# An attention and mixture-of-experts kernel: two experts of the first batch move from the step loop to the slot loop

## The chip, the cores and the metric

The kernel runs on one core of a Trainium2 chip. The metric is the device time of one execution in microseconds; the time before is the median of three runs. The profile is one further execution, recorded by the hardware profiler. Engines are named as in the profile: PE is TensorE, DVE VectorE, ACT ScalarE, POOL GpSimd, SP the engine that issues nearly all DMAs.

## The reference, cut to what matters

```python
q_assign = argmax(q_n @ c_n.T); k_assign = argmax(k_n @ c_n.T)
mask = q_assign[..., :, None] == k_assign[..., None, :]
attn = softmax(where(mask, q @ k.T / sqrt(D), -1e9)) @ v      # 4 batches, 8 heads, 768 x 64
x = attn.transpose(0, 2, 1, 3).reshape(4 * 768, 512)
P = exp(x @ w_gate - max)                                     # 3072 x 8
for _ in range(8):                                            # rows, then columns, made to sum to one
    P /= P.sum(1, keepdims=True) + 1e-9
    P /= P.sum(0, keepdims=True) + 1e-9
    P *= N / E
for e in range(8):
    out += P[:, e:e+1] * (relu(x @ w1[e]) @ w2[e])            # w1 512 x 1024, w2 1024 x 512
```

All is float32. The kernel makes the expert products from pairs of float16 numbers (a high part and the low rest), three matmuls for one product.

## The kernel before, in words

**Attention.** A `Planner` (L61) orders this part in Python while the program is traced: each piece of work is a generator that yields the engine it wants and a cost, and the ready piece with the lowest key (`KEYS`, L488, by stage and head) goes next on its engine; `PATIENCE` says how long an engine may be kept for a piece of lower key, `RELUCT` how much an alternative engine is held back. Within this part the largest weights of the first two experts are estimated too: `scan_early` (L1147) loads each matrix in pieces of 512 columns and sums absolute values on ACT (`total`, L298), and `early_weights` (L1221) makes the first two weight pairs of expert 0.

**Steps.** The first batch then runs in the loop over t at L1582: 32 steps, one for each expert and pair of 128-column blocks of the hidden layer. A step has seven positions m = 0 to 6. At each, `layer1` (L1398) makes one of the seven products of Strassen's scheme (Winograd's variant) for layer 1, 6 matmuls of 384 columns into one of two PSUM tiles `h_ps`; these two are used in turn, some twice before they come free. `layer2` (L1540) makes the plain layer 2 of the step before at positions 1 to 6, 6 matmuls of 512 columns at each, into `o_ps`, reading the weight tile `wb` of the step before. `make_w` (L1507) makes the weights of the step after, at positions 1 to 6: a scaling of the raw first matrix on ACT (L1512), sums on POOL, high parts on ACT (L1516) and low parts on POOL (L1517), at position 3 the high half of `wb` on ACT (L1499 in `second_matrix`), at position 4 the high and low parts of the sums (L1522 on ACT, L1524 on POOL), at 5 and 6 the low half of `wb` on DVE (L1502). `store_w` (L1532) writes both tiles to memory, for the later batches. Besides, one raw pair is scanned on ACT for the scales of a later expert, and from t = 8 the input of the second batch is split (`next_x`, L1346). The results of layer 1 go through `m1` (ACT, L1411), combinations on DVE (L1401), ReLU high parts `hh` on ACT (L1610) and low parts `hl` on DVE (L1613, one position later). At an expert's end `gated` (L1554) adds `o_ps` times the gate to the tile `acc`, 512 columns at a time.

The order of instructions on each engine is the order in which they are traced: `keep_order` pins it after each position. Tiles come from pools with a fixed number of buffers; a tile whose pool has none left takes a buffer whose last readers are done, so its first writer waits for them. Those that matter here:

```python
wap = pool("wap", 3)                    # L1278, first-layer weights of a pair
ps_h = pool("ps_h", 2, space=PSUM)      # L1282
wbp = pool("wbp", 3, ax)                # L1460, second-layer weights of a pair
sump = pool("sump", 1, ax)              # L1461
rawp = pool("rawp", 8, ax)              # L1463
```

**Slots.** Batches 2 to 4 run in 24 slots, one for each batch and expert, four pairs of 28 products in all. Layer 1 of slot n stands beside layer 2 of slot n - 1, which is done with seven products too (`layer2b`, L1778): 252 matmuls of 256 columns in three PSUM tiles pa, pb, pc, with evictions on DVE (`evict`, L1768, two of 256 columns for three row groups, or one). `plan_slot` (L1732) says at which position each high half (ACT, L1696), low half (DVE, L1700) and sum (POOL, L1681) is made. The weights come from memory; in the first eight slots the sums of the second matrix are made as well (`second_sums` to `second_low`, L1719).

Of the kernel before, what the change touches and what calls it, by code (L numbers as in the profile page):

```python
# [22 lines left out]
P = 128  # L23
# [37 lines left out]
class Planner:  # L61
# [6 lines left out]
    PATIENCE = {'PE': 0.0, 'ACT': 0.0, 'POOL': 0.26, 'SP': 0.0, 'DVE': 0.0}  # L68
# [96 lines left out]
def attn_moe_kernel(  # L165
# [138 lines left out]
    NP2 = NF // 2  # L304
    NI = E * NP2
# [28 lines left out]
    with ExitStack() as actx:  # L334
# [153 lines left out]
        KEYS = dict(load=-99.6, scale=-39.4, hilo=-210.9, split0=-186.4, split1=-28.7, split2=-30.4, assign=-39.2, place=-336.7, chain=-64.9, ones=-461.5, max=-25.1, rows=-30.6, exp=0, values=64.8, out=6.0, batch=29.5, group=76.9, vsum=-28.1, group0=-123.5, inputs=-41.6, first=1000)  # L488
# [3 lines left out]
        RELUCT = [4.75, -0.72, 2.33, 16.21, 0.34, 0.01, 0.02, 5.4, -0.46, 3.06, 0.07]  # L492
# [654 lines left out]
        def scan_early(e):  # L1147
            if e:
                yield ev["scales", e - 1]
            for f in range(NF):  # L1150
                yield ev["v", NF * (e + 1) - 4 + f]
                if f == 0:
                    am8 = sm.tile([P, 2, NF], F32, name="am8", bufs=1)
                for m in range(2):
                    yield SP, 0.625
                    t = sm.tile([P, 512], F32, name="scan0", bufs=1)
                    scan_load(e, f, f + 1, m, t)
                    yield plan.copied(1.1) - plan.now.time
                    yield ACT, 0.62
                    total(am8[:, m, f : f + 1], t, t)  # L1160
            am2 = sm.tile([P, 2], F32, name="am2", bufs=1)
            yield DVE, 0.15
            nc.vector.tensor_reduce(out=am2, in_=am8, axis=AX, op=ALU.max)
            yield t_x
            yield from weight_scale(e, am2, misc_tile, sm)
            t_x.put(plan)
            ev["scales", e].set(plan)

# [85 lines left out]
        for e in range(2):  # L1254
            plan.spawn(scan_early(e), urgency("values", NF * (e + 2) - 4))
# [26 lines left out]
    ps_h = pool("ps_h", 2, space=PSUM)  # L1282

# [171 lines left out]
    before = iter(())  # L1455

    with ExitStack() as ax:
# [3 lines left out]
        sump = pool("sump", 1, ax)  # L1461
        junkp = pool("junkp", 1, ax)
        rawp = pool("rawp", 8, ax)  # L1463
        accp = pool("accp", 1, ax)
# [3 lines left out]
        def load_raw(idx):  # L1468
            e, f2 = divmod(idx, NP2)
            fs = slice(f2 * 2 * P, (f2 + 1) * 2 * P)  # L1470
            t = rawp.tile([P, 2048], F32, name="raw")
            nc.sync.dma_start(out=t[:, 0:1024].rearrange("p (c f) -> p c f", c=NC), in_=w1[e, :, fs].rearrange("(c p) f -> p c f", p=P))
            nc.sync.dma_start(out=t[:, 1024:2048].rearrange("p (j m) -> p j m", j=2), in_=w2[e, fs, :].rearrange("(j p) m -> p j m", p=P))
            raws[idx] = t
# [17 lines left out]
        def first_matrix(idx):  # L1492
            raw = raws[idx][:, 0:1024]
            return raw, raw.rearrange("p (k c t f) -> p t k c f", k=2, c=KC, t=2), sump.tile([P, 4, KC, P], F32, name="s1w")
# [59 lines left out]
        def gated(e, acc):  # L1554
            gates_ = gate_values(0, e)

            def done(i, ps):
                gate = gates_[:, i : i + 1]
                if e == 0:
                    nc.vector.tensor_scalar(out=acc[:, i], in0=ps, scalar1=gate, scalar2=None, op0=ALU.mult)  # L1560
                else:
                    nc.vector.scalar_tensor_tensor(out=acc[:, i], in0=ps, scalar=gate, in1=acc[:, i], op0=ALU.mult, op1=ALU.add)
                if e == E - 1 and i % 2 == 1:
                    nc.scalar.dma_start(out=out_v[0][:, i - 1 : i + 1], in_=acc[:, i - 1 : i + 1])
# [3 lines left out]
        AHEAD = 7  # L1568
# [9 lines left out]
        acc = accp.tile([P, NT, DO], F32, name="acc")  # L1578
        scans = {i - 5: (i,) for i in range(8, NI)}
        loads = {0: (), 1: (4, 5), 2: (6, 7, 8), 3: (9, 10)}  # L1580
        loaded = {}
        for t in range(NI):  # L1582
# [317 lines left out]
```

## Time and profile before

| | before |
|---|---|
| median of 3 runs | 2285.46 us (2285.12 to 2286.17) |
| the profiled execution | 2284.72 us |
| its span, first to last instruction | 2282.8 us |
| mean granted clock of TensorE | 0.993 |
| PE busy | 2240.6 us, 98% |
| DVE, ACT, POOL busy | 1644.5, 1143.5, 1118.2 us |

A step or a slot is found in the timeline of PE by its matmuls: 384 columns into `h_ps` are layer 1, 512 columns into `o_ps` layer 2 of a step, 256 columns into pa, pb or pc layer 2 of a slot. Consecutive matmuls overlap in the records, so the distance of starts is the time that counts.

### The profile page before, as it was taken

To read this page: it belongs to the slowest core of one execution; us is meant where nothing else is said; L and a number is where in the kernel's file an instruction comes from. 1 tells how busy PE (TensorE), PEld (TensorE's weight loads), DVE (VectorE), ACT (ScalarE), POOL (GpSimd) and SP (SyncE) were. 2 spreads that over 40 slices of the span, in tenths; PEclk is the share of its full clock that TensorE was granted. 3 is DMA by queue.
4 is the path that set the end of the run, shared out by engine and by line. 5 is a ranking of instruction groups with operands and counts; after the bars stand their busy time and mean duration, and the time that the engine had idled before them with its cause. 6 is when DMAs were issued, how large, how long until landed. Compare 5 with 4: busy or idle time off the path is not lost.

```text
span 2282.8 us, 39661 instructions
## 1 busy us (share of the span) xinstructions
PE 2240.6 (98%) x15491; PEld 1459.8 (64%) x15491; DVE 1644.5 (72%) x2777; ACT 1143.5 (50%) x2107; POOL 1118.2 (49%) x997
## 2 busy tenths in 40 slices
PE   6999999999999999999999999999999999999999
PEld 3455554445555555567777777777777777777777
DVE  7988878567666766588788877776676666666666
ACT  7777786555666665354444443333334333333332
POOL 3676787845555655376566653233332333232223
PEclk7999999999999999999999999999999999999999
DMA  5345453365545543586766664544444554344433
GB/s 125 86 102 160 103 143 98 124 222 181 196 169 190 184 145 106 204 296 212 224 221 217 237 221 167 177 143 131 151 159 136 189 166 135 130 130 139 137 122 102
DMA packets 226860, 369.78 MB, mean 162 GB/s; under 512 B 73800, under 2 KB 163824, under 8 KB 226160
## 3 DMA queue, kind: packets, MB, share of 16 engines
q1 hardware_dynamic: 226240, 365.67, 50.3%
q8 instruction: 121, 1.98, 0.4%
q10 hardware_dynamic: 432, 1.57, 0.2%
q14 instruction: 67, 0.55, 0.1%
HBM read 272.22 MB, written 80.62 MB: 155 GB/s over the span
## 4 chain that ended last, share of the span: by engine, by line
PE 92%; DVE 6%; ACT 2%; issue 1%; DMA 0%; SPq 0%; DVEq 0%; ACTq 0%
PE h_ps L1387 38%; PE pb L1800 12%; PE pa L1800 8%; PE pc L1800 8%; PE av_ps L1004 5%; PE o_ps L1548 4%; PE o_ps L1549 4%; PE o_ps L1547 4%; PE max_ps L849 2%; PE exp_ps L945 2%; PE exp_ps L946 2%; DVE mrt L853 2%; PE misc_ps L1045 1%; PE misc_ps L630 1%; DVE qH L683 0%
## 5 line engine op out<-in xcount | busy, mean ns | idle before, releaser
L1387 PEld LDWEIGHTS <-wa 128*128 128x128 f16 x5376 | 525.9, 98 | 303.6 <-issue 6.2
L1800 PEld LDWEIGHTS <-ho 128*128 128x128 f16 x5940 | 580.7, 98 | 139.8 <-DVE ho L1700 2.6
L1387 PE MATMUL h_ps<-xsT,wa 128*128 128x384 f16 x3072 | 581.8, 326 | 1.2 <-DVE xsT L324 0.6
L1387 PE MATMUL h_ps<-xsB,wa 128*128 128x384 f16 x2304 | 437.8, 326 | 1.3 <-DVE B L1401 0.6
L1681 POOL TENSOR_TENSOR B<-B,B 128x768 f32<-128x768 f32 x96 | 197.2, 2057 | 468.3 <-DVE ho L1700 426.6
L1700 DVE TENSOR_TENSOR ho<-B,ho 128x768 f16<-128x768 f32 x283 | 344.6, 1218 | 0.0
L1846 ACT ACTIVATE B<-B 128x384 f32<-128x384 f32 x288 | 149.7, 520 | 371.1 <-DVE B L1401 369.8
L1800 PE MATMUL pb<-w2o,ho 128*128 128x256 f16 x2556 | 324.8, 273 | 1.0 <-DVE C L1776 1.0
L1401 DVE SCALAR_TENSOR_TENSOR u<-h_ps,m 128x384 f32<-128x384 f32 x256 | 141.4, 552 | 245.4 <-PE h_ps L1387 242.4
L1696 ACT CAST ho<-B 128x768 f16<-128x768 f32 x283 | 226.8, 824 | 15.1 <-POOL B L1681 14.4
L970 POOL TENSOR_TENSOR psum<-psum,pe 128x512 f32<-128x512 f32 x160 | 208.2, 1317 | 43.5 <-ACT pe L952 40.2
L853 DVE TENSOR_REDUCE mrt<-max_ps 128x1 f32<-128x512 f32 (+1 forms) x288 | 188.7, 682 | 42.8 <-PE max_ps L849 41.4
L1800 PE MATMUL pc<-w2o,ho 128*128 128x256 f16 x1692 | 215.9, 273 | 1.5 <-DVE ho L1700 1.2
L1800 PE MATMUL pa<-w2o,ho 128*128 128x256 f16 x1692 | 215.1, 273 | 0.0
L1681 POOL TENSOR_TENSOR B<-B,T 128x768 f32<-128x768 f32 x48 | 95.5, 1991 | 206.0 <-DVE ho L1700 206.0
L952 ACT ACTIVATE pe<-exp_ps 128x512 f32<-128x512 f32 x288 | 164.9, 597 | 57.9 <-PE exp_ps L946 52.1
L1411 ACT ACTIVATE m<-h_ps 128x384 f32<-128x384 f32 x128 | 62.6, 489 | 191.6 <-PE h_ps L1387 181.7
L1844 ACT ACTIVATE B<-h_ps 128x384 f32<-128x384 f32 x96 | 47.1, 490 | 211.4 <-PE h_ps L1387 211.4
L1549 PE MATMUL o_ps<-wb,hl 128*128 128x512 f16 x384 | 145.5, 379 | 0.0
L1548 PE MATMUL o_ps<-wb,hh 128*128 128x512 f16 x384 | 145.5, 379 | 0.0
L1547 PE MATMUL o_ps<-wb,hh 128*128 128x512 f16 x384 | 145.5, 379 | 0.0
L1610 ACT ACTIVATE hh<-c 128x384 f16<-128x384 f32 x128 | 66.9, 523 | 143.3 <-DVE c L1401 142.0
(278 smaller groups left out, 3279.6 us busy)
## 6 DMA issues: line engine op xcount, KB each, us to landing
wa<-w1d SPq DMA_DIRECT2D x98, 896.0 KB
w2o<-w2d SPq DMA_DIRECT2D x168, 512.0 KB
raw<-in_moe_w SPq DMA_DIRECT2D x60, 512.0 KB
w1d<-wa SPq DMA_DIRECT2D x30, 896.0 KB
r<-in_moe_w SPq DMA_DIRECT2D x32, 512.0 KB
w2d<-w2s SPq DMA_DIRECT2D x32, 512.0 KB
w2d<-wb SPq DMA_DIRECT2D x96, 128.0 KB
scan<-in_moe_w SPq DMA_DIRECT2D x32, 256.0 KB
```

The source lines that it names most:

```text
L853: nc.vector.tensor_reduce(out=t["mr"][:, i0 : i0 + ni, ni - 1], in_=ps.rearrange("p (x c) -> p x c", x=ni), axis=AX, op=ALU.max)
L952: nc.scalar.activation(pe, ps.rearrange("p (x c) -> p x c", x=ni), AF.Exp, scale=SCALE)
L970: (nc.gpsimd if e == POOL else nc.vector).tensor_tensor(out=st[:, o : o + N0], in0=old[o], in1=part, op=ALU.add)
L1387: nc.tensor.matmul(ps[:, 0:HB], wa[:, w_, a, c, :], x[:, x_, c, :], start=(first and s_ == 0), stop=(s_ == len(steps) - 1), skip_group_che ...
L1547: nc.tensor.matmul(po[i], hh[:, t, ti], wbh[:, t], start=(first and t == 0), stop=False)
L1548: nc.tensor.matmul(po[i], hh[:, t, ti], wbl[:, t], start=False, stop=False)
L1549: nc.tensor.matmul(po[i], hl[:, t, ti], wbh[:, t], start=False, stop=(last and t == 1))
L1681: nc.gpsimd.tensor_tensor(out=t, in0=d[a], in1=d[c], op=ALU.subtract)
L1696: nc.scalar.copy(t[:, 0], blocks[n, g][o])
L1700: nc.vector.tensor_tensor(out=t[:, 1], in0=blocks[n, g][o], in1=t[:, 0], op=ALU.subtract)
L1800: nc.tensor.matmul(ps[:, q], h[:, h_, f, q * P : (q + 1) * P], w[:, 2 * g + f, w_], start=(first and g == 0 and s_ == 0 and q % 2 == 0), s ...
L1846: rests.append(lambda: nc.scalar.activation(c, c, AF.Relu))
```

## The change

Experts 6 and 7 of the first batch become the first two of now 26 slots (`slots`), the step loop runs 24 steps. The four pairs of each of the two experts get their weights from a generator `later`, which has a raw buffer and a tile of sums of its own, takes its `wa` and `wb` tiles from the same pools `wap` and `wbp` as the steps, and is advanced at positions 0 to 5 of each step from t = 2. The scales of experts 0, 1, 6 and 7 are found in the attention part, in pieces of 1024 columns, and the numbers of the planner are others. The first batch is now summed in the four tiles of quarters that the slots use. In the last slot one high and low half move ahead by one position, and a part of pb lies in another PSUM tile.

```diff
-    PATIENCE = {'PE': 0.0, 'ACT': 0.0, 'POOL': 0.26, 'SP': 0.0, 'DVE': 0.0}
+    PATIENCE = {'PE': 0.0, 'ACT': 0.0, 'POOL': 0.36, 'SP': 0.13, 'DVE': 0.15}
...
+    STD = E - 2
+    FROM = 3
+    EARLY = (0, 1) + tuple(range(STD, E))
...
-        KEYS = dict(load=-99.6, scale=-39.4, hilo=-210.9, split0=-186.4, split1=-28.7, split2=-30.4, assign=-39.2, place=-336.7, chain=-64.9, ones=-461.5, max=-25.1, rows=-30.6, exp=0, values=64.8, out=6.0, batch=29.5, group=76.9, vsum=-28.1, group0=-123.5, inputs=-41.6, first=1000)
+        KEYS = dict(load=168.2, scale=-46.7, hilo=-287.8, split0=-114.4, split1=-46.3, split2=-43.3, assign=-14.6, place=-445.3, chain=-118.2, ones=-454.9, max=-25.6, rows=-104.8, exp=0, values=64.2, out=14.4, batch=-159.5, group=213.1, vsum=-19.7, group0=-215.1, inputs=-292.7, first=1000, scan=-0.4)
...
-        RELUCT = [4.75, -0.72, 2.33, 16.21, 0.34, 0.01, 0.02, 5.4, -0.46, 3.06, 0.07]
+        RELUCT = [25.22, -7.8, 9.65, -7.07, 0.47, 11.56, 2.41, 13.4, 0.64, 12.77, -2.71]
...
+        am8s = {e: sm.tile([P, 2, NP2], F32, name=f"am8_{e}", bufs=1) for e in EARLY}
+
+        def scan_early(m):
+            for j, e in enumerate(EARLY):
+                for f in range(NP2):
+                    yield ev["v", NP2 * j + FROM + f]
+                    yield SP, 0.8
+                    t = sm.tile([P, 1024], F32, name=f"scan{m}", bufs=1)
+                    scan_load(e, 2 * f, 2 * f + 2, m, t)
+                    yield plan.copied(1.7) - plan.now.time
+                    yield ACT, 1.05
+                    total(am8s[e][:, m, f : f + 1], t, t)
+                ev["scan", e, m].set(plan)
...
-        rawp = pool("rawp", 8, ax)
-        accp = pool("accp", 1, ax)
+        rawp = pool("rawp", 7, ax)
...
-        def gated(e, acc):
+        def gated(e):
...
+                j, q = divmod(i, 3)
+                for r, name in enumerate((("C11", "C21"), ("C12", "C22"))[j]):
+                    o, y = totals[name][:, q], ps[:, r * HD : (r + 1) * HD]
...
-        AHEAD = 7
+        AHEAD = 6
...
+        def later():
+
+            for idx in range(NB, NI):
+                e = idx // NP2
+                raws[idx] = raw_ = rawp.tile([P, 2048], F32, name="rawx", bufs=1)
+                fill_raw(raw_, idx)
+                for _ in range(7):
+                    yield
+                wa, wb = wt = w_tiles()
+                raw, A, S_ = first_matrix(idx)
+                nc.scalar.activation(raw, raw, AF.Copy, scale=s1[:, e : e + 1])
+                yield
+                sums(S_, A[:, 1, 0], A[:, 1, 1], A[:, 0, 0], A[:, 0, 1], nc.gpsimd)
+                for o, a in ((A22, A[:, 0, 1]), (slice(A11, A12 + 1), A[:, 1])):
+                    nc.scalar.copy(wa[:, 0, o], a)
+                yield
+                for o, a in ((A22, A[:, 0, 1]), (slice(A11, A12 + 1), A[:, 1])):
+                    nc.vector.tensor_tensor(out=wa[:, 1, o], in0=a, in1=wa[:, 0, o], op=ALU.subtract)
+                yield
+                second = second_matrix(idx, wb)
+                step(second)
+                yield
+                nc.scalar.copy(wa[:, 0, 3:7], S_)
+                yield
+                for o in (0, 2):
+                    nc.gpsimd.tensor_tensor(out=wa[:, 1, 3 + o : 5 + o], in0=S_[:, o : o + 2], in1=wa[:, 0, 3 + o : 5 + o], op=ALU.subtract)
+                step(second)
+                yield
+                step(second)
+                raws.pop(idx)
+                yield
+                store_w(idx, wt)
+                yield
...
-        for t in range(NI):
+        for t in range(NB):
...
                 if m:
                     step(making)
+                if m < 6 and t > 1:
+                    step(extra)
                 if m:
                     step(before)
...
-                if t == NI - 1:
-                    reload_x(1, RIGHT[m])
...
-    slots = [(b, e) for b in range(1, B) for e in range(E)]
+    slots = [(0, e) for e in range(STD, E)] + [(b, e) for b in range(1, B) for e in range(E)]
...
+                elif n == NS - 1 and (o, g) == ("T1", 1):
+                    h, l = 2, 3
...
-        if b == 1:
+        if n < E:
...
-                tiles[CHAINS[i]] = ps_y.tile([P, 4, HD], F32, name=CHAINS[i])
+                ps = ps_y.tile([P, 4, HD], F32, name=CHAINS[i])
+                tiles[CHAINS[i]] = [ps[:, q] for q in range(3)]
+                if n == NS - 1 and CHAINS[i] == "pb":
+                    tiles["pb"][2] = h_tile()[:, 0:HD]
```

## Rows read from the trace of the kernel before

**Rows 1.** The page, busy time, share of the span and instructions of each engine.

```profile
PE 2240.6 (98%) x15491; PEld 1459.8 (64%) x15491; DVE 1644.5 (72%) x2777; ACT 1143.5 (50%) x2107; POOL 1118.2 (49%) x997
```

**Rows 2.** Windows by stage: length, busy us (instructions), granted clock, DMA share, GB/s.

```profile
0.00:60.00 60.00, 39.74 (x192) 19.76 (x193) 44.12 (x106) 43.59 (x77) 21.85 (x36) 0.80 0.53 123
60.00:478.40 418.40, 407.15 (x2669) 206.08 (x2668) 329.73 (x637) 298.95 (x711) 316.50 (x381) 1.00 0.44 115
...
543.00:958.50 415.50, 415.50 (x2217) 216.64 (x2215) 261.80 (x429) 242.59 (x402) 211.96 (x220) 1.00 0.51 168
...
987.20:2249.30 1262.10, 1261.62 (x9662) 944.74 (x9661) 917.64 (x1426) 504.91 (x830) 510.82 (x307) 1.00 0.51 171
2249.30:2282.80 33.50, 27.98 (x254) 24.46 (x251) 17.72 (x34) 5.93 (x8) 15.43 (x7) 0.99 0.41 126
```

**Rows 3.** Timeline of PE, one step: start us, us, engine, line, tiles.

```profile
819.35 1.14 PE L1387 MATMUL h_ps<-xsB,wa 128*128 128x384 f16 x6
820.33 1.14 PE L1387 MATMUL h_ps<-xsT,wa 128*128 128x384 f16 x6
...
822.60 1.14 PE L1387 MATMUL h_ps<-xsB,wa 128*128 128x384 f16 x6
...
833.95 1.14 PE L1387 MATMUL h_ps<-xsB,wa 128*128 128x384 f16 x6
```

**Rows 4.** Timeline of PE, one pair of a slot, from its first product to the next.

```profile
1508.78 1.14 PE L1387 MATMUL h_ps<-xsB,wa 128*128 128x384 f16 x6
...
1522.48 1.14 PE L1387 MATMUL h_ps<-xsB,wa 128*128 128x384 f16 x6
```

**Rows 5.** Timeline of PE and of DVE in the tail, idle time before in brackets.

```profile
2256.77 1.92 PE L1800 MATMUL pc<-w2o,ho 128*128 128x256 f16 x16 [1.22 <-DVE ho L1700]
...
2278.65 0.81 PE L1800 MATMUL pb<-w2o,ho 128*128 128x256 f16 x6 [0.97 <-DVE C L1776]
...
2253.41 0.48 DVE L1776 SCALAR_TENSOR_TENSOR C<-pa,gates,C 128x256 f32<-128x256 f32 x1 [2.66 <-PE pa L1800]
```

**Rows 6.** Line 298, scans in attention and in a step; waits of PE.

```profile
L298 ACT ACTIVATE scan<-scan x32: 612/630/682, 150.0 to 371.6; 128x512 f32<-128x512 f32 x32
...
806.32 1.05 ACT L298 ACTIVATE junk<-raw 128x1024 f16<-128x1024 f32 x1
...
PE exp_ps L945 <- ACT pe L952: 3.4, 6, 1.0
```

**Rows 7.** Windows of two single steps.

```profile
804.76:819.35 14.59, 14.59 (x79) 7.62 (x78) 8.43 (x14) 8.98 (x15) 7.51 (x8) 1.00 0.46 118
...
833.95:848.54 14.59, 14.59 (x79) 7.63 (x78) 10.63 (x17) 8.98 (x15) 7.51 (x8) 1.00 0.26 92
```

**Rows 8.** Timeline of ACT in the step from 804.76 and the start of the next.

```profile
811.98 1.14 ACT L1499 ACTIVATE wb<-raw,s 128x1024 f16<-128x1024 f32 x1
...
814.74 1.03 ACT L1522 CAST wa<-s1w 128x1024 f16<-128x1024 f32 x1
816.58 0.52 ACT L1610 ACTIVATE hh<-c 128x384 f16<-128x384 f32 x1 [0.81 <-DVE c L1401]
...
820.53 0.49 ACT L1411 ACTIVATE m<-h_ps 128x384 f32<-128x384 f32 x1 [0.52 <-PE h_ps L1387]
```

**Rows 9.** Timeline of DVE in the same step.

```profile
807.45 1.01 DVE L324 SCALAR_TENSOR_TENSOR xst<-xqB,sx,xst 128x768 f16<-128x768 f32 x1
...
816.46 0.95 DVE L1613 SCALAR_TENSOR_TENSOR hl<-c,hh 128x384 f16<-128x384 f32 x1
...
818.90 0.54 DVE L1401 SCALAR_TENSOR_TENSOR c<-h_ps,u 128x384 f32<-128x384 f32 x1
...
819.84 0.74 DVE L1502 SCALAR_TENSOR_TENSOR wb<-raw,s,wb 128x512 f16<-128x512 f32 x1
```

**Rows 10.** Windows where the steps begin.

```profile
478.00:484.00 6.00, 4.08 (x25) 1.98 (x23) 4.85 (x8) 4.10 (x9) 1.40 (x2) 0.96 0.67 221
484.00:490.30 6.30, 5.73 (x31) 2.14 (x31) 4.84 (x7) 2.70 (x4) 0.00 (x0) 0.50 0.46 187
```

More of the change, by code (lines that the diff above doesn't have):

```diff
@@ L1145, in out_batch, with early_scale @@
             t_x.put(plan)
[L1147 to L1160, printed above, removed]
+        am8s = {e: sm.tile([P, 2, NP2], F32, name=f"am8_{e}", bufs=1) for e in EARLY}
[10 more added lines that the diff above has]
+                ev["scan", e, m].set(plan)
+        def early_scale(e):
+            for m in range(2):
+                yield ev["scan", e, m]
             am2 = sm.tile([P, 2], F32, name="am2", bufs=1)
             yield DVE, 0.15
-            nc.vector.tensor_reduce(out=am2, in_=am8, axis=AX, op=ALU.max)
+            nc.vector.tensor_reduce(out=am2, in_=am8s[e], axis=AX, op=ALU.max)
             yield t_x
@@ L1167, in scan_early @@
             ev["scales", e].set(plan)
+            if e != EARLY[-1]:
+                plan.spawn(early_scale(EARLY[EARLY.index(e) + 1]), plan.now.key + 100.0)
         def two_tiles():
@@ L1253, in attn_moe_kernel @@
         plan.spawn(first_x(), urgency("inputs", nheads))
-        for e in range(2):
-            plan.spawn(scan_early(e), urgency("values", NF * (e + 2) - 4))
+        for m in range(2):
+            plan.spawn(scan_early(m), urgency("scan", 8))
+        plan.spawn(early_scale(0), urgency("scan", 8))
         plan.spawn(early_weights(), urgency("values", nheads - 12))
@@ L1282, in attn_moe_kernel @@
     ps_h = pool("ps_h", 2, space=PSUM)
+    accp = pool("accb", 1)
     def h_tile():
@@ L1455, in attn_moe_kernel, with total_tile @@
     before = iter(())
+    totals = {}
+    def total_tile(name):
+        return accp.tile([P, 3, HD], F32, name=name, bufs=2 if name == "C21" else 1)
     with ExitStack() as ax:
@@ L1577, in attn_moe_kernel @@
         plan.unpin()
-        acc = accp.tile([P, NT, DO], F32, name="acc")
-        scans = {i - 5: (i,) for i in range(8, NI)}
-        loads = {0: (), 1: (4, 5), 2: (6, 7, 8), 3: (9, 10)}
+        scans = {i - 5: (i,) for i in range(8, NB)}
+        def later():
[30 more added lines that the diff above has]
+                yield
+        extra = later()
+        for name in ("C11", "C21", "C12", "C22"):
+            totals[name] = total_tile(name)
+        loads = {0: (), 1: (4, 5), 2: (6, 7, 8), 3: (9,)}
         loaded = {}
-        for t in range(NI):
+        for t in range(NB):
             e, f2 = divmod(t, NP2)
@@ L1585, in attn_moe_kernel @@
                 po = []
-            for idx in loads.get(t, (t + AHEAD,) if t + AHEAD < NI else ()):
+            for idx in loads.get(t, (t + AHEAD,) if t + AHEAD < NB else ()):
                 load_raw(idx)
-            if 0 < t < NI - 1:
+            if 0 < t < NB - 1:
                 wts[t + 1] = w_tiles()
                 making = make_w(t + 1, wts[t + 1])
-            if t + 2 >= NI:
+            if t + 2 >= NB:
                 loaded[t + 2] = load_wa((t + 2) % NI)
@@ L1648, in attn_moe_kernel @@
             wts.pop(t - 1, None)
-            before = layer2(po, hh, hl, wt, f2 == 0, f2 == NP2 - 1, gated(e, acc) if f2 == NP2 - 1 else None)
-        for x in (sink, inputs, scanning):
+            before = layer2(po, hh, hl, wt, f2 == 0, f2 == NP2 - 1, gated(e) if f2 == NP2 - 1 else None)
+        for x in (sink, inputs, scanning, extra):
             for _ in x:
@@ L1765, in attn_moe_kernel, with evict @@
     LAST = {3: ("C11", 0, 0), 4: ("C22", 1, 1), 5: ("C12", 0, 1), 6: ("C21", 1, 0)}
-    totals = {}
-    def evict(e, ps, gates_, into, begun, qs=range(3)):
+    def evict(n, e, ps, gates_, into, begun, qs):
         for q in qs:
@@ L1792, in layer2b @@
                 if name not in totals:
-                    totals[name] = accp.tile([P, 3, HD], F32, name=name, bufs=2 if name == "C21" else 1)
+                    totals[name] = total_tile(name)
             count = 0
@@ L1811, in layer2b @@
                         if count in ready:
[L1812 removed]
+                            evict(n, e, ps, gates_, INTO[i], begun, ready[count])
                         if count in ready and e == E - 1:
```

36 lines of the change are left out of this document (17 added, 19 removed).

## The prediction

> **What bounds the kernel now.** I read the share of busy time first: TensorE is busy 98% of the span, VectorE 72%, ScalarE and GpSimd half [rows 1]. Then the same by stage: from 543 to 958.5 us (first batch's steps) and from 987.2 to 2249.3 us (slots) TensorE is idle 0.0 and 0.5 us; its idle time is in the attention part, at the two joints and in the tail [rows 2]. So in steps and slots the time is the number of matmuls, and anything else costs nothing as long as it does not hold TensorE up. Third, the timeline of TensorE: a step goes from one first product to the next in 14.60 us (819.35 to 833.95) [rows 3], the same piece of a slot, one pair of column blocks, in 13.70 us (1508.78 to 1522.48) [rows 4].
>
> **What the change removes.** Two experts are eight steps, which become eight pairs in slots: 8 x (14.60 - 13.70) = **-7.2 us**. Layer 1 is the same in both; layer 2 loses an eighth of its columns. The filling and draining of the slots' two-stage order happens once, before and after. A new batch boundary now lies inside the slots; there are two there already and all idle time of that stage is 0.5 us [rows 2], so the third costs at most 0.3 us, which I take.
>
> **The tail.** TensorE waits 1.22 us in the chain pc for a low half on VectorE, which stands behind six evictions that begin at 2253.41, and 0.97 us before the last six matmuls, for the eviction of their own tile [rows 5]. The change moves that low half one place ahead, where VectorE was idle 2.66 us, and gives the third part of pb a buffer of its own. Both waits should go; of the second I keep 0.9 us, since the last eviction must still follow the one before it: **-2.1 us**. If a new wait took their place I would lose just that, so the ends are 0 and -2.2.
>
> **The attention part.** The scans for scales grow from two experts to four: 32 loads and 32 sums as before, of twice the width. A sum of 512 columns took 0.63 us, one of 1024 takes 1.05 [rows 6], so ScalarE gets 32 x 0.42 = 13.4 us more, in a stage where it is busy 299 of 418 us [rows 2]. TensorE waited for ScalarE's exponentials only 3.4 us in all [rows 6]. Keys, reluctances and patience of the planner change too, so the whole order there is new, on SP and GpSimd queues as well. That can't be costed instruction by instruction. Bounds: TensorE is idle 11.2 us from 60 to 478 us, so a better order gains at most that (the first 60 us, with 20.3 idle, could give some more); a loss is bounded by the 13.4 us if all of it lay on the chain. The nearest row, the 3.4 us, says little of it shows: I take **0**, with -6 to +6 for the range.
>
> **The weights of the two experts.** Here I see the price. Their first, low and sum parts are made by a generator that runs beside the steps from t = 2: fifteen pieces for a pair, six pieces a step, thus 2.5 steps a pair, done in step 21. The work itself has room: ScalarE is busy 9.0 us of 14.6, GpSimd 7.5, VectorE 8.4 to 10.6 [rows 7], and a pair adds about 4.1 us of ScalarE in 2.5 steps. But pool wbp keeps three tiles, and the change leaves it so. From position 3 of step t all three are taken: layer 2 of the pair t-1 reads one to the end of the step, the pair t is in the second, and t+1 is written into the third. Only at positions 0 to 2 is one free. The new pair needs a fourth tile from its piece 11 (high half, on ScalarE) until its store, piece 15. The order on each engine is fixed, so whoever comes too late holds up its whole queue.
>
> *Odd pairs of the sequence* (first, third, ...): piece 11 falls on position 4, so ScalarE waits till the last layer 2 matmul of the step. Put on the step that ends at 819.35 [rows 3, 8]: high half 1.14 us to 820.6, the queued hh 0.52 to 821.2, the new sum copy 1.03 to 822.2, the next hh to 822.7, then m1, 0.49, to 823.2. The product of position 2 adds onto the bank that m1 reads, and would have begun at 822.60 [rows 3]: **0.7 us** late. Its store is issued at position 2 of the next step, and the next regular high half then waits a little for it, under cover.
>
> *Even pairs*: piece 11 falls on position 1 and finds the free tile, but the store is piece 15, at position 5. So the regular high half at position 3 (at 811.98 in the row) finds none until about 819.5. Then ScalarE: high half to 820.6, hh to 821.2. VectorE stood meanwhile at the low part that needs this hh (816.46 in the row): that to 821.7, the low half of the weights (0.74) to 822.5, and only then the combination that frees the bank, 0.54, to 823.1 [rows 8, 9]. TensorE wanted that bank at 820.33 [rows 3]: **2.8 us** late, and 3.8 where a split of the next batch's input (1.01 us on VectorE) stands at the same position [rows 9].
>
> Four pairs of each kind: 4 x 0.7 + 4 x (2.8 to 3.8), that is 14.0 to 18.0; I take **+16 us**. No row of before shows this wait, since there the third tile always came free in time; the lower end is 0, if a cover that I don't see exists, and the upper one adds a 2.8 us stall for each odd pair as well, if the regular pair after it gets the later of two buffers: 27 to 29.
>
> **The clock.** Between 478 and 484 us TensorE was busy 4.08 of 6 us, and from 484 to 490.3 the granted clock was 0.50, the level of 1.2 GHz [rows 10]; such a dip loses half of its length, some 3.2 us. Whether single gaps of 2.8 us in dense work bring one, no row shows; the gaps of 1.22 and 0.97 us in the tail did not (0.99 there [rows 2]). Ends: none, or four, 13 us. The surroundings are denser than in that row, so I take about one, **+3 us**.
>
> A rule for pieces stands in the Trainium skill, Perfetto Trace Analysis, Optimizing Scalar/DVE Operations: where ScalarE and VectorE are not saturated but cause bubbles elsewhere, broken-up instructions may finish sooner. By it the change would come out at the first rival's time. Another section of the same page, Optimization Strategy, says that the same gap repeated on the engine that should be saturated can mean that a buffer for the next tile is missing; that is the forecast's mechanism, and no row of before shows such a gap.
>
> **Sum.** -7.2 + 0.3 - 2.1 + 0 + 16 + 3 = +10.0. The profiled execution took 2284.72 us (span 2282.8 and 1.9 around it), 0.7 under the median of 2285.46; 2284.7 + 10.0 = 2294.7, said as **2295 us**. Other work that I cost at nothing: evictions of the steps, 12 halves for 6 rows at each expert's end, on a VectorE that is busy 63% in the steps; scans of sixteen pairs instead of twenty-four; the 2.3 MB of loads and stores that each new pair adds on SP, which runs half a step ahead.
>
> **Rivals.** (a) *No buffer wait*: the pieces are at most 1.14 us, ScalarE has 5 us free a step, so they slip in; then only the gains stay: 2284.7 - 9.0 = 2275.7. For it: the flat 14.60 of all steps. Against it: four tiles alive in three buffers. It decides where the new store lands before position 3 or the high half falls after the step's end. Chance 0.20. (b) *Waits as forecast, but the new order in attention gains 6 to 11 us*: of the 11.2 us idle there most goes; 2284 to 2289, about no change. Chance 0.15. (c) *Waits also after odd pairs, and a clock dip with most stalls*: +11 and +10 on the forecast, 2305 to 2316. Chance 0.12. (d) The forecast, with attention within some us, 2289 to 2303: 0.53.
>
> **How the numbers follow.** About 0.2%, 4.6 us, is what a measurement of this kernel can tell from no change. Faster by that is below 2280.9: (a) and a little of (b), 0.21. The band to 2290.0: most of (b) and the low end of (d), 0.17. Slower: the rest, 0.62. The range goes from 2276, in the middle of (a), to 2306, which leaves out most of (c) and the lower half of (a). The likeliest case's own range is 2289 to 2303.
>
> **What would show it.** Steps 3 to 21 no longer flat at 14.60: in each five, one of about 15.3 and one of 17.4 to 18.4, with TensorE's wait put down to a VectorE combination or to m1 on ScalarE, and ScalarE's high half of wb waiting for the o_ps matmuls. Slots at 13.70; no gaps in pc and pb of the tail. I am wrong if the steps stay flat, if the first product of step 0 comes more than 6 us off 478.4, or if the granted clock falls inside the steps more than once.

## The result: slower by 1.4%, and the profile after

| | before | after |
|---|---|---|
| median of 6 runs each | 2285.29 us | 2318.82 us (2314.52 to 2320.05) |
| ratio, with its 95% interval | | 1.0144 [1.0134, 1.0154] |
| profiled execution / span | 2284.72 / 2282.8 us | 2315.78 / 2314.0 us |

The direction was forecast, the size was not: 2295 us was said, and 2318.8 lies above the range, which ended at 2306. The profiled execution after lies 3.0 us under its median, the one before 0.6 under; so the medians differ by 33.5 us, and the account below is of the 31.2 us by which the two spans differ. In the kernel after the lines have moved: layer 1 is L1398, the combinations on VectorE L1412, the high and low halves of wb L1516 and L1519, hh and hl L1665 and L1668, the stores L1553 and L1555, the new low sums L1623.

First the busy time of each engine, the page's first part, beside [rows 1]:

```profile
PE 2239.8 (97%) x15713; PEld 1481.2 (64%) x15713; DVE 1690.7 (73%) x2846; ACT 1153.2 (50%) x2095; POOL 1175.5 (51%) x1027
```

TensorE's busy time is 0.8 us less than before, the span 31.2 us more: the loss is idle time, or time at a lower clock. The windows of steps and slots (columns as in [rows 2]) say where:

```profile
543.00:882.50 339.50, 309.03 (x1599) 157.36 (x1597) 233.56 (x379) 196.58 (x321) 210.57 (x202) 0.97 0.59 196
882.50:2314.00 1431.50, 1426.34 (x10921) 1068.11 (x10919) 1029.22 (x1604) 566.22 (x930) 578.00 (x352) 1.00 0.52 172
```

The steps, where [rows 2] had not one idle microsecond from 543 us on, now have 30.5 in 339.5, at a clock of 0.97. From first product to first slot took 480.1 us before; with eight steps of 14.60 us [rows 3] less it would be 363.3, and it is 402.4 (480.08 to 882.49). Call the difference, 39.1 us, the **excess** of the steps. The rest went as forecast: the slots went from 1324.3 to 1431.5 us, 107.2 for eight pairs of 13.70 us (109.6) and a tail shorter by 2.1; the first product of step 0 came at 480.1 against 478.4. In sum +1.7 + 39.1 - 116.8 + 107.2 = +31.2.

What the steps wait for, from the waits of TensorE and from ScalarE's writes of the tile wb with what ended the idle time before them (us, times):

```profile
PE h_ps L1398 <- DVE c L1412: 24.7, 8, 8.1
PE h_ps L1398 <- DVE u L1412: 5.2, 5, 1.5
```
```profile
  DMA w2d<-wb: 49.2, 7
  PE o_ps L1566: 13.6, 5
```

ScalarE's high halves of wb, which waited for nothing before, stood idle 62.8 us: 13.6 for layer 2 of the step before, as forecast, but 49.2 for a **store** of the tile to land. Of these seven waits four, 18.9 us, are those of the regular pair after an odd one, which the forecast had as "a little", under cover; the other three, 30.3 us, come after even pairs, where the forecast had layer 2. Two steps after even pairs show the two kinds, in a timeline of the engines:

```profile
587.97 1.14 PE L1398 MATMUL h_ps<-xsB,wa 128*128 128x384 f16 x6
588.17 1.15 ACT L1516 ACTIVATE wb<-raw,s 128x1024 f16<-128x1024 f32 x1 [6.28 <-PE o_ps L1566]
591.50 1.14 PE L1398 MATMUL h_ps<-xsT,wa 128*128 128x384 f16 x6 [2.40 <-DVE c L1412]
...
661.65 1.72 DVE L1519 SCALAR_TENSOR_TENSOR wb<-rawx,s,wb 128x512 f16<-128x512 f32 x1
664.98 2.26 POOL L1623 TENSOR_TENSOR wa<-s1x,wa 128x512 f16<-128x512 f32 x2
666.81 1.14 PE L1398 MATMUL h_ps<-xsB,wa 128*128 128x384 f16 x6
667.27 0.33 SPq L1553 DMA_DIRECT2D w1d<-wa  x1
667.69 2.63 SPq L1555 DMA_DIRECT2D w2d<-wb  x3
672.65 1.15 ACT L1516 ACTIVATE wb<-raw,s 128x1024 f16<-128x1024 f32 x1 [9.53 <-DMA w2d<-wb]
674.24 0.56 DVE L1668 SCALAR_TENSOR_TENSOR hl<-c,hh 128x384 f16<-128x384 f32 x1 [10.23 <-ACT hh L1665]
676.05 2.08 PE L1398 MATMUL h_ps<-xsT,wa 128*128 128x384 f16 x6 [8.10 <-DVE c L1412]
```

In the first, at 587.97 (after the first even pair), the high half follows the last o_ps matmul, TensorE stands idle 2.40 us and the step takes 17.39, 2.8 over 14.60: the forecast's mechanism, nearly to the tenth. In the second the regular pair after an even one takes over the buffer of the *new* pair. Its wb was complete at 663.4. But its store stands behind the store of its wa, in one queue, and that waits for GpSimd's new low sums, done at 667.2. Three pieces are then issued to 670.3, the buffer is free at 672.6, the queue of ScalarE and the one of VectorE behind it start again, and TensorE has stood idle 8.10 us.

The same gap comes back every fifth step: 2.40, 8.10, 7.34 and 3.75 us at position 1 of steps 7, 12, 17 and 22. The Trainium skill (Perfetto Trace Analysis, Optimization Strategy) says that such consistent bubbles on the engine that should be saturated can mean that there is no room for the next tile; here the trace agrees, and the experiments test it.

Around the three longer gaps the clock fell, by the windows there:

```profile
671.40:681.70 10.30, 5.65 (x16) 2.41 (x17) 6.28 (x11) 5.90 (x9) 5.22 (x6) 0.50 0.97 319
756.80:763.60 6.80, 2.99 (x9) 1.38 (x10) 5.52 (x10) 6.41 (x10) 2.37 (x2) 0.50 1.04 351
845.50:848.90 3.40, 3.40 (x10) 1.28 (x9) 3.40 (x5) 1.56 (x3) 2.87 (x3) 0.50 0.42 169
```

TensorE was busy 12.0 us at 0.50, the level of 1.2 GHz, so the clock cost 6.0 us. After the gap of 2.40 us it stayed at full speed.

The tail's two waits [rows 5] are gone; the same places in the timeline of TensorE, with no idle time ahead of them:

```profile
2288.80 2.13 PE L1858 MATMUL pc<-w2o,ho 128*128 128x256 f16 x18
2290.76 1.47 PE L1858 MATMUL pb<-w2o,w2s 128*128 128x256 f16 x12
...
2308.45 1.47 PE L1858 MATMUL pb<-w2o,ho 128*128 128x256 f16 x12
2309.76 0.82 PE L1858 MATMUL h_ps<-w2o,ho 128*128 128x256 f16 x6
```

### The profile page after: what moved, and what is told of

The parts are those of the page before. It is cut to its first block, busy times and chain, and to the rows that moved or that the text cites. A ratio compares the mean times of both kernels' runs of the same rounds, so it can differ in the third digit from the quotient of the medians.

```text
span 2314.0 us, 40227 instructions
## 1 busy us (share of the span) xinstructions
PE 2239.8 (97%) x15713; PEld 1481.2 (64%) x15713; DVE 1690.7 (73%) x2846; ACT 1153.2 (50%) x2095; POOL 1175.5 (51%) x1027
## 4 chain that ended last, share of the span: by engine, by line
PE 85%; DVE 7%; ACT 2%; POOL 2%; DMA 2%; issue 1%; SPq 1%; DVEq 0%; ACTq 0%; POOLq 0%
PE h_ps L1398 34%; PE pb L1858 13%; PE pa L1858 9%; PE pc L1858 9%; PE av_ps L1007 5%; PE exp_ps L948 2%; PE max_ps L852 2%; PE exp_ps L949 2%; PE o_ps L1564 2%; PE o_ps L1565 2%; PE o_ps L1566 2%; DVE mrt L856 1%; DVE wb L1519 1%; DMA w2d<-wb 1%; PE misc_ps L1048 1%
## 5 line engine op out<-in xcount | busy, mean ns | idle before, releaser
L1398 PEld LDWEIGHTS <-wa 128*128 128x128 f16 x5376 | 526.3, 98 | 327.6 <-issue 24.0
L1858 PEld LDWEIGHTS <-ho 128*128 128x128 f16 x6444 | 630.3, 98 | 148.5 <-DVE ho L1754 0.8
L1398 PE MATMUL h_ps<-xsT,wa 128*128 128x384 f16 x3072 | 583.8, 327 | 30.5 <-DVE c L1412 24.2
L1735 POOL TENSOR_TENSOR B<-B,B 128x768 f32<-128x768 f32 x104 | 215.7, 2076 | 522.9 <-DVE ho L1754 479.4
L1398 PE MATMUL h_ps<-xsB,wa 128*128 128x384 f16 x2304 | 437.6, 326 | 2.4 <-ACT m L1422 1.3
L1754 DVE TENSOR_TENSOR ho<-B,ho 128x768 f16<-128x768 f32 x307 | 374.9, 1221 | 4.9 <-ACT ho L1750 4.9
L1858 PE MATMUL pb<-w2o,ho 128*128 128x256 f16 x2748 | 349.7, 273 | 0.0
L1412 DVE SCALAR_TENSOR_TENSOR u<-h_ps,m 128x384 f32<-128x384 f32 x256 | 141.3, 552 | 214.0 <-PE h_ps L1398 213.8
L1750 ACT CAST ho<-B 128x768 f16<-128x768 f32 x307 | 246.3, 825 | 18.1 <-POOL B L1735 17.4
L1858 PE MATMUL pa<-w2o,ho 128*128 128x256 f16 x1836 | 233.4, 273 | 0.0
L1412 DVE SCALAR_TENSOR_TENSOR B<-h_ps,u 128x384 f32<-128x384 f32 x208 | 114.8, 552 | 48.9 <-PE h_ps L1398 48.1
L1007 PE MATMUL av_ps<-pe,vn 128*64 128x512 f32 (+1 forms) x768 | 134.4, 492 | 0.0
L949 PE MATMUL exp_ps<-qX 98*128 98x256 f16 (+1 forms) x384 | 120.4, 328 | 0.0
L1735 POOL TENSOR_TENSOR T<-B,B 128x768 f32<-128x768 f32 x52 | 109.5, 2107 | 4.1
```

What stands on the lines that cost most here:

```text
L949: nc.tensor.matmul(o, t["k2"][0:98, ki], t["qa"][0:98, a:z], start=False, stop=True)
L1007: nc.tensor.matmul(av[o, a:z], vn[:, i, :], heads[t]["pe", c][:, i - i0], start=(i == 0), stop=False, skip_group_check=True)
L1398: nc.tensor.matmul(ps[:, 0:HB], wa[:, w_, a, c, :], x[:, x_, c, :], start=(first and s_ == 0), stop=(s_ == len(steps) - 1), skip_group_che ...
L1412: nc.vector.scalar_tensor_tensor(out=t, in0=ps[:, 0:HB], scalar=KAPPA, in1=x, op0=ALU.mult, op1=ALU.add)
L1735: nc.gpsimd.tensor_tensor(out=t, in0=d[a], in1=d[c], op=ALU.subtract)
L1750: nc.scalar.copy(t[:, 0], blocks[n, g][o])
```

## The experiments

**A first set asks whether the tile wb is the cause.** All four edit `later`, the generator of the new weights.

*e1_own_wb*: the new pairs get a fourth tile wb of their own. (To make room in SBUF, two small constants are built in a pool of the attention part; e2, e5, e6 and e8 to e11 have that too.)

```diff
-                wa, wb = wt = w_tiles()
+                wa, wb = wt = wa_tile(), wbp.tile([P, 2, 2, DO], F16, name="wbx", bufs=1)
```

> The generator gets a second-layer weight tile of its own beside the three of the steps (two constants of the attention part move to a pool that is freed, to make room). Theory S, the missing fourth tile is the whole loss in the steps: every step from 4 on 14.60 us but for a few tenths, the 24 steps to the first slot shorter by 39 us than in the changed kernel (402.4 to about 363.5 us), no high half of wb waiting for a store or for layer 2; total 2277 us, 2274 to 2281. Rival L, the steps are long because three engines and the DMA queue have a quarter more work per step: at least 10 us of the 39 stay, total 2287 or more. Rival A, the new order in attention loses: the first product of step 0 would have to come 20 us or more later than before; it came 2.0 us later.

*e2_own_wb_even*: the same for the even pairs of the sequence alone.

> Only the even pairs (second, fourth, ...) of the sequence get a tile of their own; the odd pairs still share the three. By my prediction's steps the odd pairs cost 0.7 us each when the high half waits for the end of layer 2, so 2277 + 3 = 2280 us, 2277 to 2286. A rival, odd and even pairs cost alike: 2277 + 20 = 2297 us.

*e3_named*: three buffers as in the change, but each pair's buffer named by hand, so that the regular pair after an even one takes the buffer that layer 2 has just left. This is what the prediction assumed.

> The three tiles of wb are named by hand, so that after an even pair the regular tile takes the buffer that layer 2 gives up at the end of the step, and not the one that the new pair's store gives up (after an odd pair as in the changed kernel). That is the choice that my prediction assumed. If only this choice was wrong: 0.7 us after each odd and 2.8 to 3.8 after each even pair, 14 to 18 us in all, every wait of a regular high half put down to o_ps matmuls, total 2277 + 16 = 2293 us, 2289 to 2299, and no or one clock dip in the steps. If the shortage costs as much whoever waits: 2310 us or more.

*e4_short*: three buffers, 12 pieces a pair instead of 15. The high half stands at position 0 of a step, both low halves and the store of wb at position 1.

> Three tiles as in the changed kernel, but the pieces come in another order and 12 to a pair, two steps: the high half at position 0 of the second step, both low halves and the store at position 1, the first-layer parts after that. The tile is then taken for about 2 positions and its store about 3.5 us instead of 4 positions and the store. Theory S in its stricter form (what counts is that the tile is out of use by position 3): steps at 14.6 to 15, total 2277 to 2283 us. If three buffers are too few however they are used: 2290 us or more.

Each ratio is to the kernel before, run beside it, with a 95% interval; steps and excess are read from one profiled execution of each kernel. The medians of e2 and e3 are of three and two executions.

| | median, us | ratio to before | steps, us | excess |
|---|---|---|---|---|
| after | 2318.82 | 1.0144 [1.0134, 1.0154] | 402.4 | 39.1 |
| e1_own_wb | 2293.41 | 1.0041 [1.0026, 1.0055] | 379.6 | 16.3 |
| e2_own_wb_even | 2294.77 | 1.0044 [1.0028, 1.0060] | 381.5 | 18.2 |
| e3_named | 2301.47 | 1.0076 [1.0056, 1.0097] | 388.5 | 25.2 |
| e4_short | 2298.80 | 1.0068 [1.0053, 1.0083] | 387.2 | 23.9 |

The fourth buffer takes 22.8 us of the excess away, and ScalarE's idle time before the high halves to nothing. So the shortage is the larger part. The theory wanted 2277, however: 16 us stayed, with another cause; by its number that is rival L, which the second set takes up. From e1 to e2 the steps grow by 1.9 us, 0.5 for each odd pair, where 0.7 was forecast; the intervals of the two overlap, so the totals don't tell this from nothing. Nor does it lie where the forecast had it: the wait for m1 at position 2 is seen once (0.33 us in step 19), and what e2 has and e1 has not are waits one step later, at position 1 of steps 10, 15 and 20, after the regular high half has waited for the odd pair's store. e3 shows what my own assumption would have given: the steps after the even pairs take 17.39, 18.90, 19.62 and 17.15 us, 2.6 to 5.0 over 14.60, where I had 2.8 to 3.8. In its trace, ScalarE's writes of wb, with what ended the idle time before them:

```profile
  PE o_ps L1571: 32.8, 8
  DMA w2d<-wb: 19.1, 4
```

That is layer 2 first and the store second, the reverse of the kernel after: all four regular halves after even pairs now wait for layer 2, and the store's waits that are left are those after odd pairs. So which buffer is taken over decides between some 4 and some 8 us in each of the last three steps after even pairs. Of the 22.8 us, 13.9 go with that choice (after to e3) and 8.9 with the missing buffer (e3 to e1).

e4 nearly removes the shortage without a fourth buffer (ScalarE idle 4.4 us in all before wb) and is still not told from e3. So its 2298.80 us, which is in the range of "too few however they are used", is hardly the buffers' doing. What TensorE waits for there, and what stands on VectorE just ahead of such a combination c:

```profile
PE h_ps L1398 <- DVE c L1412: 15.6, 11, 3.7
```
```profile
591.03 2.07 DVE L1615 TENSOR_TENSOR wa<-rawx,wa 128x256 f16<-128x256 f32 x2
```

These are the new pair's low parts of the first matrix, which the new order puts at position 5. The low halves of wb at position 1 stand ahead of the combination u instead, and its waits are 1.9 us in two.

**What stayed in e1** is seen in its waits of TensorE, and in two places of its timeline:

```profile
PE h_ps L1398 <- DVE u L1412: 9.7, 7, 2.4
PE h_ps L1398 <- DVE c L1412: 3.2, 4, 1.7
```
```profile
548.55 1.21 DVE L1519 SCALAR_TENSOR_TENSOR wbx<-rawx,s,wbx 128x512 f16<-128x512 f32 x1
549.68 0.54 DVE L1412 SCALAR_TENSOR_TENSOR u<-h_ps,m 128x384 f32<-128x384 f32 x1
550.28 1.14 PE L1398 MATMUL h_ps<-xsT,wa 128*128 128x384 f16 x6 [0.94 <-DVE u L1412]
...
701.58 2.77 SPq L1555 DMA_DIRECT2D w2d<-wbx  x3
704.47 0.93 SPq L1336 DMA_DIRECT2D amw<-am  x1
711.49 0.34 SPq L1339 DMA_DIRECT2D all<-amw  x1
717.35 0.42 DVE L1343 TENSOR_REDUCE gmax<-all 128x2 f32<-128x256 f32 x1 [4.52 <-DMA all<-amw]
```

First place: on VectorE the new low half stands ahead of the combination u that frees a bank. Second place, in one step: the maxima for the next scale (amw) go to memory right behind the new pair's stores. They are issued 8.7 us into the step, as soon as VectorE has made them, and 8.1 us into it in before. But the load that brings them back, and waits for them to land, follows 7.02 us later, and 3.05 in before:

```profile
696.06 0.33 SPq L1325 DMA_DIRECT2D amw<-am  x1
699.11 0.33 SPq L1328 DMA_DIRECT2D all<-amw  x1
```

The windows from the one to the other, e1 first; the last two numbers are the DMA engines' share and GB/s:

```profile
704.47:711.49 7.02, 7.02 (x40) 3.64 (x38) 4.27 (x6) 3.02 (x5) 4.13 (x4) 1.00 1.00 234
696.06:699.11 3.05, 3.05 (x19) 1.65 (x17) 0.56 (x1) 1.76 (x3) 0.94 (x2) 1.00 0.06 6
```

The DMA engines are full with the new pair's stores and the next loads, where in before they stood nearly idle. VectorE waits 4.52 us for the maxima with everything queued behind, and TensorE 2.45 us after that. Both places depend on where the new pieces stand, so the next set moves them.

**A second set moves the new pieces.** *e5_order* is e1 with the pieces at positions 2 to 6, ten a pair, from t = 3; the generator is regrouped for that (two idle pieces for six, sums and high parts apart, the sums' high and low parts together, low halves and store last), and the lines below show only where it is advanced. The low halves of wb then come at 2 and 3, behind u, and the stores fall in the steps in which SP carries no maxima.

```diff
-                if m < 6 and t > 1:
+                if m > 1 and t > 2:
                     step(extra)
```

> As the kernel with the fourth tile, and the pieces in another order: at positions 2 to 6 only, ten to a pair, so exactly two steps, with the low halves of wb at positions 2 and 3 behind the combination u2 of VectorE and the stores in odd steps, away from the even ones in which SP carries an expert's scales. Theory Q, what was left after the fourth tile (16.9 us over flat steps) is the order in VectorE's and SP's queues at the beginning of a step: steps from 4 on within 0.3 us of 14.60, the 24 steps 363 to 366 us, total 2276 to 2280 us, faster than before. Rival L, too much work on VectorE and GpSimd per step: 10 us or more stay, total 2286 or more.

*e6_order_even* is the same, one step later (`t > 3`): the stores meet the maxima.

> The same, one step later, so that the stores of the new pairs stand in the steps in which SP also carries an expert's scales (6, 10, 14, 18). If SP's order is what made steps 11, 15 and 19 long with the fourth tile: 2 to 4 us more than the kernel one step earlier in each of the steps after these, 4 to 10 us in all, with VectorE waiting for the load of the scales. If the low halves on VectorE did it: the same as the kernel one step earlier, within 2 us.

e5_order took 2281.82 us against 2284.81 for the kernel before beside it, 0.9991 [0.9982, 1.0001], with 369.2 us in the steps, an excess of 5.9. So order cost e1 10.4 us. e6_order_even took 2298.42 (two executions), and 17.6 us more in the steps: the theory's sign, and well over its size. Its waits of VectorE, of TensorE and of ScalarE:

```profile
DVE gmax L1343 <- DMA all<-amw: 9.2, 4, 3.8
```
```profile
PE h_ps L1398 <- ACT m L1422: 8.7, 6, 3.3
```
```profile
ACT rawx L1618 <- DMA rawx<-in_moe_w: 14.3, 6, 3.7
```

VectorE's wait for the scale is there, as the theory said, but TensorE loses only 1.0 us behind it (its waits for u). The large waits, for m, have another cause: m stands on ScalarE behind the scaling of the next raw pair, which waits for that pair's load (step 13: idle 3.70 us until 692.44, m at 693.49, TensorE at 694.01 after 3.26 us). Around three of the gaps the granted clock fell to 0.50 besides, which it did nowhere in e5 from step 4 on; TensorE was busy 11.7 us at it, so some 5.8 us of the 17.6 are the clock's. So e6 shows that one step's shift costs 17.6 us, and not that the scale does. What is left in e5_order lies in steps 9, 11 and 19 (15.80, 16.40, 16.11 us). Step 11, on GpSimd and VectorE:

```profile
648.70 2.25 POOL L316 TENSOR_TENSOR tx<-xqB,xqB 128x768 f32<-128x768 f32 x1
649.22 2.16 DVE L1672 SCALAR_TENSOR_TENSOR hl<-c,hh 128x384 f16<-128x384 f32 x1
650.92 2.57 POOL L1633 TENSOR_TENSOR wa<-s1x,wa 128x512 f16<-128x512 f32 x2
651.74 0.67 DVE L1344 TENSOR_SCALAR gmax<-gmax 128x2 f32<-128x2 f32 x1
652.45 1.08 DVE L1345 TENSOR_SCALAR gmax<-gmax 128x2 int32<-128x2 int32 x1
654.01 0.55 DVE L1412 SCALAR_TENSOR_TENSOR u<-h_ps,m 128x384 f32<-128x384 f32 x1
```

While GpSimd works, hl takes 2.16 us (0.54 where GpSimd stands still, as at 711.16 in e1), and two operations on two numbers a row 0.67 and 1.08 us (0.17 in the kernel before). To test whether that running side by side makes the rest, *e9_late_sums* moves GpSimd's new low sums from position 6 to position 2 of the next step:

```diff
+                    step(second)
+                    for o in (0, 2):
+                        nc.gpsimd.tensor_tensor(out=wa[:, 1, 3 + o : 5 + o], in0=S_[:, o : o + 2], ...
...
                 nc.scalar.copy(wa[:, 0, 3:7], S_)
-                for o in (0, 2):
-                    nc.gpsimd.tensor_tensor(out=wa[:, 1, 3 + o : 5 + o], in0=S_[:, o : o + 2], ...
```

> e5_order with GpSimd's two low parts of the new sums (2.57 us) moved from position 6 to position 2 of the next step, so that they no longer run beside VectorE's hl and the tiny operations of the scale (stretched to 2.16 and 1.08 us in step 11 of e5_order). Theory (sharing between GpSimd and VectorE costs the steps 9, 11 and 19): the excess of the 24 steps falls from 6.5 to 3 to 4.5 us, total 2278.5 to 2280.5. Rival (it only moves the collision to the regular low parts behind it on GpSimd, which wait 2.6 us longer): excess 6.5 or more, total 2281.5 or above.

It took 2324.35 us, 1.0172 [1.0158, 1.0186]: slower than the change itself, for eight pairs of operations moved by three positions. Neither theory had this mechanism. The waits of SP and of ScalarE, and one place in the timeline:

```profile
SPq L1553 <- POOL wa L1605: 64.8, 7, 12.1
```
```profile
ACT rawx L1620 <- DMA rawx<-in_moe_w: 38.2, 7, 9.4
```
```profile
638.43 2.26 POOL L1605 TENSOR_TENSOR wa<-s1x,wa 128x512 f16<-128x512 f32 x2
640.72 0.33 SPq L1553 DMA_DIRECT2D w1d<-wa  x1
641.14 2.62 SPq L1555 DMA_DIRECT2D w2d<-wbx  x3
643.82 0.48 SPq L1490 DMA_DIRECT2D rawx<-in_moe_w  x1
648.22 1.15 ACT L1620 ACTIVATE rawx<-rawx,s 128x1024 f32<-128x1024 f32 x1 [4.53 <-DMA rawx<-in_moe_w]
649.28 0.47 ACT L1422 ACTIVATE m<-h_ps 128x384 f32<-128x384 f32 x1
```

The low sums end at 640.69. Only then can SP issue the store, and the load of the *next* raw pair stands behind it, though it needs nothing of the sums. It lands late, ScalarE waits for it, and m waits behind ScalarE. *e10_load_first* is e9 with the load ahead of the store; *e11_order_load_first* is e5 with that alone:

```diff
-                    store_w(idx - 1, wt)
-                e = idx // NP2
-                raws[idx] = raw_ = rawp.tile([P, 2048], F32, name="rawx", bufs=1)
-                fill_raw(raw_, idx)
+                if idx < NI:
+                    e = idx // NP2
+                    raws[idx] = raw_ = rawp.tile([P, 2048], F32, name="rawx", bufs=1)
+                    fill_raw(raw_, idx)
+                if wt:
+                    store_w(idx - 1, wt)
```

> e9_late_sums with the load of the next raw pair issued ahead of the store of the last one, and nothing else. In e9_late_sums SP waited 64.8 us in 7 for the late low sums before the store, and ScalarE 38.2 us in 7 for the load queued behind it. Theory (the order on SP's queue made all of e9_late_sums' loss): these waits of ScalarE and the gaps of 2.9 to 6.1 us at m go, the 24 steps take 366 to 369 us, total 2278 to 2282. Rival (GpSimd's later low sums hold the steps up by themselves): over 2290.

> e5_order with the load of the next raw pair issued ahead of the store of the last one, and nothing else. In e5_order that store waits for little, so the theory of the queue says about no change: 2280.5 to 2283. Rival (load and store share more than the queue, or the store's later issue makes the scales behind it late): over 2285.

| | median, us | ratio to before | steps, us | excess |
|---|---|---|---|---|
| e5_order | 2281.82 | 0.9991 [0.9982, 1.0001] | 369.2 | 5.9 |
| e6_order_even | 2298.42 | 1.0060 [1.0040, 1.0080] | 386.8 | 23.5 |
| e9_late_sums | 2324.35 | 1.0172 [1.0158, 1.0186] | 413.1 | 49.8 |
| e10_load_first | 2285.80 | 1.0004 [0.9995, 1.0013] | 372.2 | 8.9 |
| e11_order_load_first | 2281.75 | 0.9988 [0.9979, 0.9997] | 368.1 | 4.8 |

The load ahead of the store is worth 40.9 us in the steps of e9; ScalarE's waits for the load are gone in e10, which still ends between its theory and its rival. With the queue's part out of the way, e10 answers e9's own question: later sums don't help, 372.2 against 368.1 in e11. In step 12 GpSimd's regular low parts hold TensorE up 1.90 us, which e11 has not, so e9's rival is seen there. e5 and e11 are the best versions seen, 2281.82 and 2281.75 us, and not told apart, as expected. e11 stood against 2284.73 beside it; its interval lies just under one, a gain smaller than the 0.2% that the prediction counts as a difference.

**A third set takes the other two parts.** *e7_tail* is the kernel before with the last slot's edits alone; *e8_planner* is e5_order with the planner's old numbers (and the new key `scan`, which the old ones lack).

> The kernel before with the change to the last slot alone (a high and a low half one position ahead, a third part of pb in another PSUM tile). My prediction's term: both waits of TensorE gone, 2.1 us less, total 2282 where before is 2284. Rival, new waits take their place: no difference.

> The kernel with the fourth tile and the other order of pieces, but with the planner's keys, reluctances and patience of the kernel before (and the new key of the scans). The first product of step 0 comes at 480 to 482 us with the new numbers and at 478.4 in the kernel before. If the wider scans cost the attention part something and the new numbers win it back: 3 to 10 us later than with the new numbers. If the new numbers are the loss: at 478 us or earlier, and as much less in total.

e7_tail: 2283.20 us, 0.9990 [0.9981, 1.0000]; its slots take 1322.1 us against 1324.3, and both gaps are gone. That is the term of -2.1 us, at the edge of what repeats can tell. e8_planner: 2289.28 us, 1.0021 [1.0011, 1.0031], 7.5 more than e5_order. Its first product comes at 479.4 us, but its first step takes 25.2 us against 16.3, with the last matmuls of attention among the first products of the step. So the new numbers are needed to carry the larger scans; they gain nothing over the kernel before.

## Why the prediction was right or wrong

**Right.** The slots: eight pairs of 13.70 us are 109.6, and they grew by 107.2; the rest, -2.4, is near the tail's -2.1. The tail: -2.1, shown alone in e7_tail. The mechanism of the even pairs, four tiles alive in three buffers, and its first instance (2.8 us over 14.60 in step 7, as worked out).

**Right in size only.** Attention was taken as 0, and the first product moved by 1.7 us, inside the 6 allowed; in e7_tail, with the attention part of before, it moved by 1.6 as well, so nothing of it is shown to be the change's. That is luck: the larger scans cost 7.5 us under the old numbers (e8 to e5), the new numbers win just that back, and the forecast named a bound for either and costed neither. The odd pairs, 0.5 us each for 0.7, are not told from nothing by the totals, and the wait for m1 at position 2 that gave the 0.7 hardly came.

**Wrong, first: "the work itself has room"**, and with it the list costed at nothing ("SP, which runs half a step ahead"). With no buffer missing (e1), 16.3 us of excess stay, for a term of 0. Busy shares gave room: ScalarE 9.0 of 14.6 us. But room over a step says nothing of *where* in a queue a piece stands. Order alone cost 10.4 us (e1 to e5), 17.6 when e5's pieces stand one step later (e6), and 40.9 between e9 and e10. I had followed the new high half through the queues of ScalarE and VectorE, but the new low halves and low parts, the loads and the stores through none. The last 4.8 to 5.9 us (e11, e5), in steps 11 and 19 for the most part, stay open: VectorE's operations stretched beside GpSimd's, and the queue of GpSimd, are both seen there, and e10 shows only that moving the sums is no cure. The 1.1 us by which e11's steps are shorter than e5's are not shown to be the load's: they lie in step 9 (14.69 against 15.80), e8, with e5's order, has 14.71 there, and the medians are the same to 0.1 us.

**Wrong, second: which buffer.** The step that failed is "finds none until about 819.5", the end of layer 2. I let the regular pair take the buffer that layer 2 leaves; from the second even pair on it took the new pair's, which came free later. I had that thought, but for the odd pairs, as an end of the range and only with another 2.8 us. The row shows why it is 8: the store of wb waits in SP's queue behind the store of wa, which waits for GpSimd, and then it has to land. The four steps after even pairs lost 2.8, 11.0, 9.0 and 5.6 us, 28.3 with the clock, where the forecast had 11.2 to 15.2. With the assumed choice made by hand (e3_named) they lost 14.7, within that; in e1, with no wait for a buffer, the same four lose 2.9, by order.

**How much each is worth.** The steps took 39.1 us too much where 19 were forecast, 16 for the waits and 3 for the clock. A fourth buffer takes away 22.8 of them, near the 19, but by two errors that cancel: with the choice that I assumed the shortage adds only 8.9 us to what order costs anyway, and the choice that was made adds 13.9. The 16.3 that are left are the larger part of the miss. The parts don't add up simply: step 15 takes 18.89 us in e1, but 14.59 in e3 and 14.80 in the kernel after, where the stall of step 12 went before. No run has three buffers in e5's order, so what the shortage costs by itself stays open.

**Wrong, third: the number of dips.** The term was "about one dip", 3 us; three dips cost 6.0. The text had said that more than one dip would prove it wrong. The excess over 3 goes with the choice of buffer: with the assumed one (e3) the clock fell twice, for 3.41 us each, which cost 3.4.

**The rivals.** (a), no buffer wait, had the same blind spot: e1 has no buffer wait and takes 2293, not 2276. The rule for broken-up instructions named beside it (the Trainium skill, Perfetto Trace Analysis, Optimizing Scalar/DVE Operations) did not decide here: the pieces are small, their engines unsaturated, and the steps of e1 and e5 differ by 10.4 us with instructions of the same size in another order. (c) was nearest. Its waits after odd pairs did come on ScalarE, 18.9 us of them, but TensorE felt them only as 0.24 and 1.60 us in steps 10 and 20; the dips came with three of the stalls.

## What to carry to other kernels

For each tile of a pool, write down who holds it until when, the store's landing included, and then ask which buffer the next writer gets: the sum over lifetimes says that a stall comes, the choice says how long it is. When work is added to a pinned order, go through each queue (also the DMA-issuing one) and name the instruction directly behind each new one and what it feeds; free busy time does not answer that. On a queue in order, put loads that depend on nothing ahead of stores that wait for a late engine.

## What the runs showed of the hardware that was not expected

The clock: TensorE's granted clock fell to 0.50 around single gaps of 8.10, 7.34 and 3.75 us in dense work, not at one of 2.40. But in e1 it stood at 0.50 from 720.1 to 723.5, behind a gap of 2.45 that ended at 719.27, and in e6 from 672.5 to 675.9, around a gap of 1.87 that ended at 672.91 and came 0.8 us after one of 0.56. So the length of the gap alone does not tell, and no run isolated it. While GpSimd worked, VectorE's low half of wb took 1.64 us instead of 0.74 (e1 at 709.13 and 711.63), and an operation on 128 x 2 numbers 1.08 instead of 0.17 (e5 at 652.45, and before), the most in proportion. The Trainium skill (GPSIMD Engine Reference, Specifications) says that GpSimd shares its SBUF interfaces with VectorE, and names instructions with two SBUF inputs among those that contend; the trace agrees for the low half, which has two. The operation on 128 x 2 numbers has one, and no run isolates why it stretched. The last piece of a store of wb was issued by 670.32, and the buffer was free for ScalarE 2.3 us later.
